# Output matmuls in two PSUM banks by column halves, with a second weight chunk kept on chip and 32-wide transposes

## The chip, the cores and the metric

The kernel runs on one core of a Trainium2 chip. The metric is the device time of one execution in microseconds (us); less is better. The engines of the core are TensorE (PE; its weight loads are listed apart as PEld), VectorE (DVE), ScalarE (ACT), GpSimd (POOL) and SyncE (SP). They run side by side and wait for each other on semaphores. SP and POOL issue the DMA transfers of this kernel's main loop.

## The reference

Two independent parts, whose outputs stand side by side. Part A is a long convolution through Fourier transforms; the change does not touch it. Part B is attention with a recurrent memory over 64 segments of 32 rows:

```
mem = mem0                                   # 8 rows of 1024
for s in range(64):
    h = concat(mem, x[32*s : 32*s+32])       # 40 rows
    q, k, v = h @ Wq, h @ Wk, h @ Wv         # 32 heads of 128
    p = softmax(mask(q @ k.T * scale))       # per head
    o = (p @ v) @ Wo                         # 40 rows of 1024
    mem, out[s] = o[:8], o[8:]
```

All four weights are 1024 x 4096 or 4096 x 1024 in bf16, 8 MB each, and each segment needs the memory rows that the segment before has produced. So every segment passes over all of the weights, and segments can't overlap.

## The kernel before

Part A and the work of part B that does not depend on the memory come first: keys, queries and values of the last 8 of each segment's 32 rows are prepared for all segments and left in DRAM (`REC`, `VBD`); the loop multiplies 32 rows by the K, Q and V weights, 8 of the memory and the segment's first 24. Then the loop over the 64 segments runs in an order written out by hand (`tc.manual_schedule()`), so each engine executes its instructions as the program lists them.

In a segment, the weights come as 64 chunks of 128 x 2048 (`order`): 8 each for K, Q, K, Q of the two groups of heads (`g`), 16 for V, and 16 for the output (`Wo`, one for each two heads). 47 of the chunks stay in SBUF; the other 17 (`STREAM`, places in `order`) are read from a DRAM copy `WS` through a ring of 6 buffers (`wring`). `done(ch)` frees a buffer after its last matmul and `fetch()` issues the next load on SP's queue. Two of the 17 are helped by unused columns of PSUM (`KEPT`): "A", an output chunk, lies there whole from the first segment on and is copied back quarter by quarter by VectorE (`quarter`, L817); "B", a key chunk, lies there to five eighths, is copied into its ring buffer by `move` (L800), and has its other three eighths loaded (L721).

The steps of one segment, in TensorE's order:

- `fill_mem` transposes the first half of the old output `Y` (L862) and VectorE copies its 8 memory rows into `hT` (in the tile `rec`, L863). Four key chunks follow, then the second half of `fill_mem`, then the other four.
- `Proj.run` (L918) multiplies a chunk: four matmuls of 512 columns, each with a 32-column stationary operand, side by side in four column tiles of the array. `evac` (L927, ScalarE) copies the result to SBUF as `qkv_sb` in a single buffer "rot".
- `transposes` (L933) turns a 128 x 512 result with four 128 x 128 transposes, and VectorE or ScalarE copies the result into `KT` or `QT`. `scores`, `softmax_a`, `softmax_b` and `attend` follow.
- `out_proj` and `project` (L1002) multiply with Wo: a chunk is four matmuls of 512 columns with a 64-column stationary operand, two side by side, all into one PSUM bank `yacc`, which takes its turn with the accumulators of the projections in a pool of two.
- ScalarE copies `yacc` to `Y` in two halves (L1078), and POOL writes the output rows to DRAM with two transfers (L1080).

The pool `one` has a single buffer for each tag. The tag "PT" is held in turn by `PT` (the transposed probabilities, read by `attend`) and by `Y`. The tag "QT" is held by `QT`, by the attention output `OT` of the first group and by every second quarter of A.

POOL also issues the load of the next segment's `rec` (L856, after the last projection) and of `VBs` (L889), and copies small operands for the scores (L893, L900).

Of the kernel before, what the change touches and what calls it, by code (L numbers as in the profile page):

```python
# [20 lines left out]

STREAM = (0, 5, 10, 15, 21, 26, 31, 36, 41, 46, 49, 52, 54, 57, 60, 61, 63)
KEPT = {14: "A", 4: "B"}
K0_ORDER = (0, 1, 4, 5, 2, 3, 6, 7)
# [3 lines left out]
X_LOAD = 1  # L28
RING = 6
LATE_SLOT = 4  # L30

# [385 lines left out]
def b_kernel(ctx: ExitStack, tc, x, mem0, Wq, Wk, Wv, Wo, outb, n_seg, run_a):  # L417
    nc = tc.nc
# [15 lines left out]
    for g in range(2):  # L434
        order += [(2, kc, g) for kc in range(8)]
    for hp in range(16):
        order.append((3, hp, 0))
# [257 lines left out]
    def more(i):  # L695
# [9 lines left out]
    loads = [(s, ch) for s in range(n_seg) for ch in order_s  # L705
             if s == 0 and ch not in v_temp[2:] or s > 0 and kept.get(ch) != "A"]
    live = {}
# [8 lines left out]
    def fetch():  # L716
        if loads:
            s, ch = loads.pop(0)
            live[s, ch] = k, t = slot()
            if s > 0 and ch in kept:  # L720
                nc.sync.dma_start(t[:, 0:768], stream_src(ch)[:, 0:768])  # L721
                move(kept[ch], t, True)
            else:
                nc.sync.dma_start(t[:], stream_src(ch))

# [13 lines left out]
    with c0p:  # L739
# [16 lines left out]
        for g in range(2):  # L756
# [14 lines left out]
            if g == 0:  # L771
                with tc.issue_after(got[-1].ins):
                    place_late(4, stage_home)
                    for i in [*range(len(v_temp) - 2, n_more), *range(len(v_temp) - 2)]:
                        place_late(1, lambda: more(i))
                    place_late(1, lambda: pw(2))
                    place_late(4, stage_home)
        assert len(late) == len(at_hand)

# [11 lines left out]
    OTi, tpi = OTp[:].bitcast(I32), tps[:].bitcast(I32)  # L791
    homes = {"B": [(OTi[:, :, 416:512], slice(384, 768)), (tpi[:, 1, :], slice(768, 1024))]}

    def move(name, t, back):
        for p, cols in homes[name]:
            w = t[:].bitcast(I32)[:, cols]
            if len(p.shape) == 3:
                w = w.rearrange("p (b x) -> p b x", b=4)
            src, dst = (p, w) if back else (w, p)
            nc.vector.tensor_scalar(out=dst, in0=src, scalar1=0, scalar2=None, op0=ALU.bitwise_or)  # L800

# [3 lines left out]
    def keep(ch):  # L805
        t = live[0, ch][1]
        if kept[ch] == "A":
            w = t[:].bitcast(I32).rearrange("p (hh dh f x) -> p hh f dh x", hh=2, dh=2, f=2)
            for q in range(4):
                nc.vector.tensor_scalar(out=OTi[:, q, 160:416].rearrange("p (dh x) -> p dh x", dh=2),  # L810
                                        in0=w[:, q // 2, q % 2], scalar1=0, scalar2=None, op0=ALU.bitwise_or)
        else:
            move(kept[ch], t, False)

    def quarter(q):
        t = one.tile([128, 512], BF, tag=("rot", "QT")[q % 2], name="quarter")
        nc.vector.tensor_scalar(out=t[:].bitcast(I32), in0=OTi[:, q, 160:416], scalar1=0, scalar2=None,  # L817
                                op0=ALU.bitwise_or)
        return [(o, o + 256, t[:, 256 * dh:256 * dh + 256]) for dh, o in enumerate(quarter_cols(q))]
# [14 lines left out]
    def done(ch):  # L834
        if now[0] == 0 and ch in at_hand:
            place_late(1, at_hand[ch][1])
        elif ch in streamed and (now[0] == 0 or kept.get(ch) != "A"):
            if now[0] == 0 and ch in kept:
                keep(ch)
            free.append(live.pop((now[0], ch))[0])  # L840
            i = order_s.index(ch)
            if now[0] == 0 and i == LATE_SLOT:
                free.append(2)
                fetch()
            fetch()
# [8 lines left out]
    def load_x(s):  # L854
        rec = one.tile([128, 768], BF, tag="rec", name="rec")
        nc.gpsimd.dma_start(rec[:], REC[:, s, :])  # L856
        pend[s] = (rec[:, 0:256].rearrange("p (k t) -> p k t", k=8), rec[:, 256:512], rec[:, 512:768])

    def fill_mem(hT, Y, half):
        tp = tps[:, 0, :]  # L860
        for j in (2 * half, 2 * half + 1):
            nc.tensor.transpose(tp[:, j * 128:(j + 1) * 128], Y[:, j * 128:(j + 1) * 128], ident[:])  # L862
        nc.vector.tensor_copy(  # L863
            hT.rearrange("p (dh j) t -> p dh j t", dh=2)[:, :, 2 * half:2 * half + 2, 0:NM],
            tp.rearrange("p (j dh r) -> p dh j r", j=4, dh=2)[:, :, 2 * half:2 * half + 2, 0:NM])

    with tc.manual_schedule():
        for _ in range(RING - 3):
            fetch()
# [14 lines left out]
        for s in range(n_seg):  # L884
# [19 lines left out]
            class Proj:  # L904


                def __init__(self, m, g):
                    self.m, self.g, self.kc = m, g, 0
                    self.acc = ps_acc.tile([128, 512], F32, tag="acc", name="acc")

                def run(self, n=8):
                    for n_kc in range(self.kc, self.kc + n):
                        kc = K0_ORDER[n_kc] if (self.m, self.g) == (0, 0) else n_kc
                        ch = (self.m, kc, self.g)
                        w = pieces(ch)
                        for c in range(4):
                            for x, y, r in columns(w, 512 * c, 512 * c + 512):
                                nc.tensor.matmul(self.acc[32 * c:32 * c + 32, x - 512 * c:y - 512 * c],  # L918
                                                 lhsT=hT[:, kc, :], rhs=r, start=(n_kc == 0 and x == 512 * c),
                                                 stop=(n_kc == 7), tile_position=(0, 32 * c))  # L920
                        done(ch)
                    self.kc += n
# [7 lines left out]
            def transposes(sb):  # L930
                tp = tps[:, 0, :]
                for i in range(4):
                    nc.tensor.transpose(tp[:, i * 128:(i + 1) * 128], sb[:, i * 128:(i + 1) * 128], ident[:])  # L933
                return tp.rearrange("p (i c r) -> p i c r", i=4, c=4)
# [59 lines left out]

            def project(h, w, OT):
                k = 40 * (h % 16)
                m = min(64, 640 - k)
                lhsT = OT[:].rearrange("p c i q -> p (c i q)")[:, k:k + m]
                for dh in range(2):
                    o = (h % 2) * 1024 + dh * 512  # L1000
                    for x, y, r in columns(w, o, o + 512):
                        nc.tensor.matmul(yacc[64 * dh:64 * dh + m, x - o:y - o], lhsT=lhsT,  # L1002
                                         rhs=r, start=(h == 0 and x == o), stop=(h >= 30),
                                         tile_position=(0, 64 * dh), skip_group_check=(h == 31))

            def out_proj(hps, OT):
                for hp in hps:
                    ch = (3, hp, 0)
                    if s > 0 and kept.get(ch) == "A":
                        continue  # L1010
                    w = pieces(ch)
                    for hh in range(2):
                        project(2 * hp + hh, w, OT)
                    done(ch)

            def out_quarter(q, w):
                hp = [ch[1] for ch in kept if kept[ch] == "A"][0]
                project(2 * hp + q // 2, w, OT1)

            fill_mem(hT, Y, 0)  # L1020
            k0 = Proj(0, 0).run(4)
            fill_mem(hT, Y, 1)
            k0 = k0.run(4).evac()
            q0 = Proj(1, 0).run(4)
# [3 lines left out]
            q0 = q0.run(4).evac()  # L1028
            k1 = Proj(0, 1).run(4)
            QT0 = one.tile([128, 4, 4, 32], BF, tag="QT", name="QT")  # L1030
            nc.vector.tensor_copy(QT0[:], transposes(q0))
            k1 = k1.run(4).evac()
            scores(0, QT0, KT0)
# [20 lines left out]
            V1 = pv1.evac()  # L1054
            yacc = ps_acc.tile([128, 512], F32, tag="acc", name="yacc")
            out_proj(range(0, 5), OT0)
            attend(1, PT1, V1)
            OT1 = evac_o(1)
            if s == 0:
                out_proj(range(5, 8), OT0)  # L1060
                out_proj(range(8, 16), OT1)
            else:
                w0 = quarter(0)
                out_proj(range(5, 8), OT0)
                w1 = quarter(1)
                out_quarter(0, w0)
                out_proj(range(8, 10), OT1)
                w2 = quarter(2)
                out_quarter(1, w1)
                out_proj(range(10, 12), OT1)  # L1070
                w3 = quarter(3)
                out_quarter(2, w2)
                out_proj(range(12, 14), OT1)
                out_quarter(3, w3)
                out_proj(range(14, 16), OT1)
            Y = one.tile([128, 512], BF, tag="PT", name="Y")
            for half in range(2):
                nc.scalar.copy(Y[:, 256 * half:256 * half + 256], yacc[:, 256 * half:256 * half + 256])  # L1078
            for dh in range(2):
# [73 lines left out]
```

## Time and profile before

| | |
|---|---|
| median of 3 runs | 1904.04 us (1904.03 to 1904.1) |
| the profiled execution | 1907.36 us, with a span of 1905.6 us from first to last instruction |
| granted TensorE clock over the span | 0.982 |
| TensorE busy | 1749.0 us, 92% of the span |
| VectorE, ScalarE, GpSimd busy | 853.8, 674.8 and 342.8 us |
| DMA | 678.00 MB, mean 356 GB/s; 373 GB/s from 600 us on |

The loop over the segments takes the span from about 450 us to the end. A profile row names the line, the engine, the operation, the tiles (out<-in), the count and times. In the chain of work that ended last, each row gives a start, a duration and what ran, and "issue" is time in which the engine waited for nothing that the profile shows. In the timeline, a row's second number is the time from the start of its first instruction to the end of its last; ends of matmuls are modelled and overlap the next one, so distances are read from start to start. In brackets stands the engine's idle time ahead of it and what ended that. In the rows of DMA issues, the last number is the median time from issue to landing.

### The profile page before, as it was taken

To read this page: it belongs to the slowest core of one execution; us is meant where nothing else is said; L and a number is where in the kernel's file an instruction comes from. 1 tells how busy PE (TensorE), PEld (TensorE's weight loads), DVE (VectorE), ACT (ScalarE), POOL (GpSimd) and SP (SyncE) were. 2 spreads that over 40 slices of the span, in tenths; PEclk is the share of its full clock that TensorE was granted. 3 is DMA by queue.
4 is the path that set the end of the run, shared out by engine and by line. 5 is a ranking of instruction groups with operands and counts; after the bars stand their busy time and mean duration, and the time that the engine had idled before them with its cause. 6 is when DMAs were issued, how large, how long until landed. Compare 5 with 4: busy or idle time off the path is not lost.

```text
span 1905.6 us, 62245 instructions
## 1 busy us (share of the span) xinstructions
PE 1749.0 (92%) x26353; PEld 831.1 (44%) x26353; DVE 853.8 (45%) x2812; ACT 674.8 (35%) x1195; POOL 342.8 (18%) x1014
## 2 busy tenths in 40 slices
PE   6989986778999999999999999999999999999998
PEld 3433322333444444444444444444444444444444
DVE  9927863202344444444444444444443444444443
ACT  6945640112333333333333333333333333333333
POOL 4003341000121111111121111111111111111111
PEclk9999998989999999999999999999999999999999
DMA  9989889998999999999999999999999999999998
GB/s 338 351 302 329 291 271 333 327 284 277 349 373 374 373 378 373 377 372 373 373 373 378 373 376 372 370 372 372 379 374 369 371 378 374 375 373 371 372 379 311
DMA packets 251211, 678.00 MB, mean 356 GB/s; under 512 B 74850, under 2 KB 82930, under 8 KB 250932
## 3 DMA queue, kind: packets, MB, share of 16 engines
q1 hardware_dynamic: 178692, 604.26, 85.0%
q0 software_dynamic: 17488, 46.70, 7.0%
q10 hardware_dynamic: 54752, 23.07, 4.5%
q8 instruction: 206, 3.38, 0.7%
q14 instruction: 73, 0.60, 0.1%
HBM read 618.35 MB, written 59.24 MB: 356 GB/s over the span
## 4 chain that ended last, share of the span: by engine, by line
PE 80%; DMA 7%; DVE 5%; issue 4%; ACT 2%; POOL 0%; ACTq 0%; SPq 0%; DVEq 0%; POOLq 0%
PE acc L918 38%; PE yacc L1002 22%; PE kb_ps L625 5%; PE tps L933 4%; DMA wring<-WS 3%; PE vb_ps L765 3%; DMA REC<-stage 2%; PE OTp L980 1%; ACT s_sb L243 1%; DVE rec L863 1%; PE SB L942 1%; PE tps L862 1%; PE s_ps L241 1%; DMA REC<-xt 1%; PE SB L939 1%
## 5 line engine op out<-in xcount | busy, mean ns | idle before, releaser
L918 PEld LDWEIGHTS <-rec 128*32 128x32 bf16 x12288 | 283.6, 96 | 300.2 <-DVE rec L863 60.7
L927 ACT CAST qkv_sb<-acc 128x512 bf16<-128x512 f32 x384 | 224.7, 585 | 480.0 <-PE acc L918 287.9
L1002 PEld LDWEIGHTS <-OT 128*64 128x64 bf16 x4348 | 255.1, 109 | 195.3 <-ACT OT L992 27.6
L918 PE MATMUL acc<-wring,rec 128*32 128x512 bf16 x2556 | 252.7, 382 | 22.8 <-DVE rec L863 19.1
L918 PE MATMUL acc<-Wres,rec 128*32 128x512 bf16 x3328 | 249.4, 380 | 0.6 <-issue 0.6
L1002 PE MATMUL yacc<-wring,OT 128*64 128x512 bf16 (+1 forms) x1540 | 235.9, 380 | 5.0 <-DMA wring<-WS 4.9
L918 PE MATMUL acc<-Wmid,rec 128*32 128x512 bf16 x3072 | 234.4, 382 | 0.0
L1002 PE MATMUL yacc<-Wmore,OT 128*64 128x512 bf16 (+1 forms) x1280 | 185.4, 381 | 0.0
L817 DVE TENSOR_SCALAR quarter<-OTp 128x256 int32<-128x256 int32 x252 | 101.1, 422 | 187.6 <-ACT OT L992 149.3
L1080 POOL DMA_DIRECT2D out_dram<-Y x128 | 63.7, 502 | 484.5 <-ACT Y L1078 484.2
L918 PE MATMUL acc<-pw,rec 128*32 128x512 bf16 x1796 | 144.8, 382 | 0.1
L1078 ACT CAST Y<-yacc 128x256 bf16<-128x256 f32 x128 | 41.4, 375 | 274.5 <-PE yacc L1002 274.5
L992 ACT CAST OT<-OTp 128x640 bf16<-128x640 f32 x128 | 88.6, 692 | 129.7 <-PE OTp L984 129.0
L918 PE MATMUL acc<-Wlate,rec 128*32 128x512 bf16 x1280 | 104.0, 384 | 17.1 <-DVE rec L863 17.1
L948 DVE TENSOR_REDUCE mx<-SB 128x5 f32<-128x200 f32 x128 | 47.1, 368 | 153.4 <-PE SB L942 153.3
L856 POOL DMA_DIRECT2D rec<-REC x64 | 36.2, 566 | 405.0 <-PE acc L918 372.1
L1002 PE MATMUL yacc<-Wlate,OT 128*64 128x512 bf16 x768 | 105.7, 383 | 0.2 <-ACT OT L992 0.2
L933 PEld LDWEIGHTS <-qkv_sb 128*128 128x128 bf16 x1024 | 57.8, 97 | 109.5 <-ACT qkv_sb L927 108.0
L933 PE MATMUL tps<-ident,qkv_sb 128*128 128x128 bf16 x1024 | 101.6, 222 | 0.4 <-ACT qkv_sb L927 0.3
L893 POOL COPY KT<-rec 128x128 bf16<-128x128 bf16 x128 | 38.2, 298 | 329.4 <-PE SB L942 324.2
L863 DVE COPY rec<-tps 128x32 bf16<-128x32 bf16 x128 | 22.3, 175 | 165.1 <-PE tps L862 115.8
L1027 DVE COPY KT<-tps 128x512 bf16<-128x512 bf16 x64 | 27.1, 424 | 152.2 <-PE tps L933 152.2
(215 smaller groups left out, 2392.9 us busy)
## 6 DMA issues: line engine op xcount, KB each, us to landing
wring<-WS SPq DMA_DIRECT2D x961, 512.0 KB, 6.0
rec<-REC POOLq DMA_DIRECT2D x64, 192.0 KB, 5.8
wring<-WS SPq DMA_DIRECT2D x63, 192.0 KB
SK<-s_sb SPq DMA_DIRECT2D x16, 512.0 KB, 4.8
SU<-s_sb SPq DMA_DIRECT2D x16, 512.0 KB, 4.9
Kg<-SK SPq DMA_DIRECT2D x32, 256.0 KB, 4.2
Ug<-SU SPq DMA_DIRECT2D x32, 256.0 KB, 5.7
REC<-stage ACTq DMA_DIRECT2D x16, 512.0 KB, 10.9
```

Of the source, the lines that this page charges most:

```text
L625: nc.tensor.matmul(ps[:], lhsT=ws[kc][:, hl * 128:(hl + 1) * 128], rhs=xbt(kc).rearrange("p s t -> p (s t)"), start=(kc == 0), stop=(kc == 7))
L765: nc.tensor.matmul(ps[:], lhsT=xbt(kc)[:, 16 * tb:16 * tb + 16, :].rearrange("p s t -> p (s t)"), rhs=ws[kc][:, c * 512:(c + 1) * 512], st ...
L817: nc.vector.tensor_scalar(out=t[:].bitcast(I32), in0=OTi[:, q, 160:416], scalar1=0, scalar2=None, op0=ALU.bitwise_or)
L863: nc.vector.tensor_copy(hT.rearrange("p (dh j) t -> p dh j t", dh=2)[:, :, 2 * half:2 * half + 2, 0:NM], tp.rearrange("p (j dh r) -> p dh ...
L918: nc.tensor.matmul(self.acc[32 * c:32 * c + 32, x - 512 * c:y - 512 * c], lhsT=hT[:, kc, :], rhs=r, start=(n_kc == 0 and x == 512 * c), st ...
L927: nc.scalar.copy(sb[:], self.acc[:])
L933: nc.tensor.transpose(tp[:, i * 128:(i + 1) * 128], sb[:, i * 128:(i + 1) * 128], ident[:])
L948: nc.vector.tensor_reduce(out=mx[:], in_=S, op=ALU.max, axis=AX.X)
L992: nc.scalar.copy(OT[:], o_view)
L1002: nc.tensor.matmul(yacc[64 * dh:64 * dh + m, x - o:y - o], lhsT=lhsT, rhs=r, start=(h == 0 and x == o), stop=(h >= 30), tile_position=(0, ...
L1078: nc.scalar.copy(Y[:, 256 * half:256 * half + 256], yacc[:, 256 * half:256 * half + 256])
L1080: nc.gpsimd.dma_start(bass.AP(outb.tensor, outb.offset + SEG * s * 2048 + 512 * dh, [[2048, 32], [1, 512]]), Y[64 * dh + NM:64 * dh + 40, :])
```

## The change

- *Output in two banks.* `yacc` becomes two tiles of the same pool of two, one for each half of the 512 columns. Each output matmul has 256 columns. The first four chunks and the last four run half by half: all four with the first half (f = 0), then all four with the second. `Y`'s first half is copied after the last four chunks' f = 0.
- *Handover.* The next segment's `fill_mem` half 0 is issued before the last chunk's f = 1. Half 1 comes after three key chunks instead of four.
- *32-wide transposes.* `turn_tile` does a 128 x 128 transpose as four, each in one of the four column tiles. `fill_mem` and `transposes` use it.
- *Chunks.* 48 chunks are resident instead of 47; the new one takes a buffer of the ring, which now has 5. 16 are streamed in the first segment; after that both kept chunks lie in PSUM (B with a quarter of a quarter in an SBUF tile `B_rest`), so that 14 are loaded per segment. B is no longer copied into a ring buffer: VectorE copies four parts of it (`quarter_b`) into the tags "PT", "QT", "PT" and "rot", and they are multiplied as four pieces between the other chunks of the second key projection.
- Between two quarters of A stands one output chunk instead of two. The places in `STREAM` and the order of the output chunks (`O_ORDER`) differ, and the copy of `QT0` moves from VectorE to ScalarE.

```diff
-STREAM = (0, 5, 10, 15, 21, 26, 31, 36, 41, 46, 49, 52, 54, 57, 60, 61, 63)
-KEPT = {14: "A", 4: "B"}
+STREAM = (1, 7, 13, 18, 20, 24, 30, 35, 41, 46, 49, 53, 56, 59, 60, 62)
+KEPT = {13: "A", 4: "B"}
+FIRST, LAST = (0, 1, 2, 3), (15, 11, 12, 14)
+O_ORDER = (*FIRST, 4, 5, 6, 7, 8, 9, 10, 13, *LAST)
-RING = 6
+RING = 5
...
+        place_late(1, lambda: base.tile([128, 2048], BF, tag="wring2", name="Wring"))
...
+    B_rest = one.tile([128, 4, 32], I32, name="B_rest")
+    B_homes = [tpi[:, 1, :].rearrange("p (c x) -> p c x", c=4),
+               SB[:].bitcast(I32)[:, 200:456].rearrange("p (c x) -> p c x", c=4),
+               OTi[:, :, 416:480], OTi[:, :, 480:512]]
+    def bits(dst, src):
+        nc.vector.tensor_scalar(out=dst, in0=src, scalar1=0, scalar2=None, op0=ALU.bitwise_or)
+    def quarter_b(q, tag):
+        n = 64 if q < 3 else 32
+        t = one.tile([128, 4, 2 * n], BF, tag=tag, name="quarter_b")
+        bits(t[:].bitcast(I32), B_homes[q])
+        w = [(512 * c + 128 * q, 512 * c + 128 * q + 2 * n, t[:, c, :]) for c in range(4)]
+        if q == 3:
+            w += [(512 * c + 448, 512 * c + 512, B_rest[:].bitcast(BF)[:, c, :]) for c in range(4)]
+        return w
...
+    def turn_tile(dst, src):
+        for e in range(0, 128, 32):
+            nc.tensor.matmul(dst[e:e + 32, :], lhsT=src[:, e:e + 32], rhs=ident[:], start=True, stop=True,
+                             is_transpose=True, tile_position=(0, e))
...
-            def project(h, w, OT):
+            def project(h, f, w, OT, stop=False):
...
-                    o = (h % 2) * 1024 + dh * 512
-                    for x, y, r in columns(w, o, o + 512):
-                        nc.tensor.matmul(yacc[64 * dh:64 * dh + m, x - o:y - o], lhsT=lhsT,
+                    o = (h % 2) * 1024 + dh * 512 + f * 256
+                    for x, y, r in columns(w, o, o + 256):
+                        nc.tensor.matmul(yacc[f][64 * dh:64 * dh + m, x - o:y - o], lhsT=lhsT,
...
-            fill_mem(hT, Y, 0)
-            k0 = Proj(0, 0).run(4)
+            if s == 0:
+                fill_mem(hT, Y, 0)
+            k0 = Proj(0, 0).run(3)
             fill_mem(hT, Y, 1)
-            k0 = k0.run(4).evac()
+            k0 = k0.run(5).evac()
...
-            k1 = Proj(0, 1).run(4)
+            k1 = Proj(0, 1)
+            if s > 0:
+                kb = [ch[1] for ch in kept if kept[ch] == "B"][0]
+                b0, b1 = quarter_b(0, "PT"), quarter_b(1, "QT")
+                k1.run(1)
+                k1.add(kb, b0)
+                b2 = quarter_b(2, "PT")
+                k1.run(2)
+                k1.add(kb, b1)
+            else:
+                k1.run(4)
             QT0 = one.tile([128, 4, 4, 32], BF, tag="QT", name="QT")
-            nc.vector.tensor_copy(QT0[:], transposes(q0))
-            k1 = k1.run(4).evac()
+            nc.scalar.copy(QT0[:], transposes(q0))
+            if s > 0:
+                b3 = quarter_b(3, "rot")
+                k1.run(3)
+                k1.add(kb, b2)
+                k1.add(kb, b3)
+            k1 = k1.run(8 - k1.kc).evac()
...
-            yacc = ps_acc.tile([128, 512], F32, tag="acc", name="yacc")
-            out_proj(range(0, 5), OT0)
+            yacc = [ps_acc.tile([128, 512], F32, tag="acc", name="yacc") for f in range(2)]
+            for f in range(2):
+                for hp in FIRST:
+                    out_half(hp, f, OT0)
+            out_proj((4,), OT0)
...
             Y = one.tile([128, 512], BF, tag="PT", name="Y")
-            for half in range(2):
-                nc.scalar.copy(Y[:, 256 * half:256 * half + 256], yacc[:, 256 * half:256 * half + 256])
+            for f in range(2):
+                for hp in LAST:
+                    if f == 1 and hp == LAST[-1] and not last:
+                        fill_mem(pend[s + 1][0], Y, 0)
+                    out_half(hp, f, OT1, hp == LAST[-1])
+                nc.scalar.copy(Y[:, 256 * f:256 * f + 256], yacc[f][:, 0:256])
```

## The prediction

> **What bounds the kernel now.** I read the granted clock first (0.982 over the span, 1.00 in the segment loop), then the chain of work that ended last, cut to one segment (22.5 us; 64 of them take three quarters of the span).
>
> ```profile
> 1041.91 0.39 PE yacc L1002 x3
> 1042.30 0.89 issue
> 1043.19 0.19 DVE rec L863
> ...
> 1043.42 1.05 PE acc L918 x16
> 1044.46 0.23 PE tps L862 x2
> ...
> 1044.72 0.18 DVE rec L863
> ...
> 1044.95 1.91 PE acc L918 x32
> 1046.86 0.33 PE tps L933 x4
> ```
>
> Nearly everything in it is TensorE (PE). It stands still only where a segment hands over to the next: output out of PSUM, transpose, copy into the stationary operand (`rec`), twice. The timeline gives issue times:
>
> ```profile
> 1041.72 0.62 PE L1002 MATMUL yacc<-wring,OT 128*64 128x512 bf16 x4
> 1042.38 0.65 ACT L1078 CAST Y<-yacc 128x256 bf16<-128x256 f32 x2 [4.20 <-PE yacc L1002]
> 1043.32 1.00 POOL L1080 DMA_DIRECT2D out_dram<-Y  x2 [7.33 <-ACT Y L1078]
> 1046.47 0.39 PE L918 MATMUL acc<-Wmid,rec 128*32 128x512 bf16 x4
> 1046.79 0.40 PE L933 MATMUL tps<-ident,qkv_sb 128*128 128x128 bf16 x4
> 1047.12 0.61 PE L918 MATMUL acc<-Wmid,rec 128*32 128x512 bf16 x8
> 1061.22 0.30 PE L1002 MATMUL yacc<-quarter,OT 128*64 128x256 bf16 x2
> 1061.33 0.62 PE L1002 MATMUL yacc<-Wmore,OT 128*64 128x512 bf16 x4
> 1061.76 0.62 PE L1002 MATMUL yacc<-wring,OT 128*64 128x512 bf16 x4
> ```
>
> Pairs of 512 columns are 0.215 us apart (x4 in 0.43), four 32-wide ones 0.217. A chunk issued at 1046.47 should be followed at 1046.69; the transposes come at 1046.79: 0.10 us lost where the array's tiling changes. Then the DMA answers: the loop from 600 us on, and the last microseconds, where nothing else is moved.
>
> ```profile
> wring<-WS SPq DMA_DIRECT2D x860, 512.0 KB, 6.0
> out_dram<-Y POOLq DMA_DIRECT2D x114, 32.0 KB, 4.8
> out_dram<-Y POOLq DMA_DIRECT2D x2, 32.0 KB, 1.7
> ```
>
> SP's queue takes 94.7% of the engines there, yet TensorE waits for a load 2.6 us in all from 500 to 1900: TensorE bounds, the DMA is close behind. An output write lands 4.8 us after its issue in this traffic (5.4 at most from 1000 to 1500), 1.7 alone.
>
> **Part by part, per segment.** *Handover.* The last pair is issued at 1041.94 (second of the x4), so the next chunk was due at 1042.16 and comes at 1043.42: 1.26 us. The second transposes delay it again: due at 1043.42 + 4 x 0.217 = 1044.29, issued at 1044.95: 0.66. Together 1.92. In the changed order the first half of `Y` is copied while the second half's matmuls run. Left are: `fill_mem` half 0 among the last matmuls (two groups of four transposes, 0.06 each, and two changes of tiling, 0.10 each: 0.31); the change to the keys, 0.10; half 1, 0.11, and the wait for its copy: the old one resumed 0.55 after its transposes began, the new one needs some 0.45 and has 0.11 + one chunk (0.22) to do: 0.12. Sum 0.64. The second copy of `Y` (0.375) and its hand-over lie under the three chunks of `run(3)`, 0.65; gone, they would cost up to 0.6. Gain 1.28.
>
> *32-wide transposes.* The four of L933 hold TensorE from 1046.69 to 1047.12, 0.43. As 16 in four column tiles, the tiling of the matmuls around, they are four groups of 0.057 ((0.33 - 0.10)/4): 0.23. Gain 0.20 x 4 = 0.80. That the transpose flag alone costs no such change no row shows; bounds 0 and 0.80, and I take 0.80, because entering the attention and output tilings (no flag) costs the same 0.10.
>
> *Column halves.* 64 pairs of 256 columns for 32 of 512. The row is the quarter: 1061.22 to 1061.33, 0.11 against 0.1075 for half a pair; at most 0.15 in sum, and I take 0.05. The second bank is the one of `V1`: its first matmul comes 8 x 0.108 = 0.87 after the first half's, the copy of `V1` (1057.45 to 1058.03, with the first output matmul at 1057.28) and its hand-over end 0.81 after: covered by 0.06. [...]
>
> *Chunk B from PSUM.* 20 small matmuls for 4: +0.02. Four DVE copies of about 0.42 replace two (0.56, 0.41); behind the first, the second is done 0.42 later and needed two chunks (0.43) later, and the fourth, which waits for the transposes to free its buffer, comes some 0.05 late. The quarters of A lie closer: between two stand a chunk and a pair, 0.54, where a copy (0.42) with its drain and hand-overs takes about 0.6: +0.05. Moving the `QT0` copy to ScalarE lies under the rest of `k1`. Together, with what the halves cost, some 0.2. TensorE's gain is 1.28 + 0.80 - 0.20 = 1.88, and 0.07 more: the mean segment is 22.59 (first to last output write), the common one 22.52, and the waits between them belong to the tight loads.
>
> *A new wait.* `quarter_b(0)` writes the buffer of `Y` (tag PT), and so waits on VectorE until both output writes have landed. Before, PT's next writer came 5 us later (softmax). Queued behind it on VectorE are the other quarters and softmax; TensorE waits for it in `k1`, and the `k1` copy on ScalarE waits for TensorE. Call E the issue of the segment's first key matmul. TensorE needs the quarter after 17 chunks (3.69), transposes (0.23) and half 1 (0.23): E + 4.15. The last pair is issued at E - 0.21; the copy of `Y` starts 0.33 after (1041.94 to 1042.38, less the shorter stream) and takes 0.375: E + 0.50. POOL issues 0.29 later (1043.03 to 1043.32), its second write 0.5 after that: E + 1.29. With a landing time W, the quarter's 0.41 and two hand-overs of 0.06, it is ready at E + 1.82 + W. TensorE waits W - 2.33.
>
> So a segment changes by W - 2.33 - 1.95 = W - 4.28 us. W is what decides. Bounds: 1.7 (alone) and 5.4 (longest). Loads in flight now: 6.0 landing over 22.5/15.4 = 1.46 per load, 4.1. In the changed order the ring has five slots and 14 loads per segment, and around E three are in flight (slots of order places 60 and 62 and of the second key chunk, freed at about E - 1.0, E - 0.6, E + 0.4; the one before, at E - 3.3, has landed). In proportion W = 1.7 + 3.1 x 3/4.1 = 4.0, which I take. With 1.5 loads ahead it is 2.8, with as many as now 4.8 to 5.0. [...] The row of 4.8 shows two loads' worth of delay, so the sum keeps the rows' proportion.
>
> *Loads.* 14 x 0.524 + 0.33 MB = 7.67 MB per segment at the 373 GB/s of the page: 20.6 us, the same as TensorE without the wait (22.59 - 1.95 = 20.6). The loads bind only if the wait vanishes. The 48th resident chunk costs one more load in the first segment, and saves a staging copy: zero, give or take 3 us in all.
>
> **Sum.** 63 x (4.0 - 4.28) = -18 us. The profiled execution took 1907.4 (span 1905.6 and 1.8 around), 3.3 above the median. 1907.4 - 18 - 3.3 = **1886**.
>
> **Rivals.** *The output write decides* (slower): W stays as now, 4.95 for the second write; 63 x 0.67 = +42, 1946. For it: the writes still fall into a burst of loads. Against: fewer in flight. It decides from W = 4.34. *No wait*: W at or below 2.3; then 20.6 per segment, -123, 1781. For it: 1.7 alone; against: the burst at E. *The flag keeps the tiling change*: three of the four blocks lie behind the wait, 3 x 0.20 x 63 = +38 on the forecast, 1924.
>
> **Chances.** Forecast 0.58 (W from 2.8 to 4.3: of it 0.06 within 0.2%), first rival 0.22 (0.01 within), second 0.10, third 0.10 (0.01 within). Faster 0.62, same 0.08, slower 0.30; 0.2%, 3.8 us, is about what a measurement of this kernel can tell from no change. The forecast's own range is W 2.8 to 4.3: 1811 to 1905. The range to 8 in 10 leaves out the second rival and W above 5: 1815 to 1946.
>
> **What would show it.** Right: a group of VectorE `quarter_b` copies whose idle time ends with the landing of out_dram, some 1.7 us a time, TensorE waiting for `quarter_b` as much; transposes of 0.23 with no 0.10 ahead; no pause at the handover above 0.2; pairs of 256 columns 0.108 apart. Wrong: no idle time ahead of `quarter_b` (then 1781), or more than 2.1 (then slower); 0.10 around the new transposes; halves at 0.13 or more (64 x 0.02 x 63 = +80).

## The result and the profile after

| | before | changed kernel |
|---|---|---|
| median | 1904.07 us | 2167.44 us (2158.81 to 2180.83, 4 runs) |
| ratio to before | | 1.138 (1.132 to 1.144) |
| profiled execution, its span | 1907.36, 1905.6 us | 2180.83, 2179.1 us |
| granted clock, span | 0.982 | 0.911 |
| mean segment in the profiled run | 22.59 us | 26.85 us |

The prediction said 1886 us, 1815 to 1946. The kernel became slower, by more than the range allowed. In the profiled run 4.26 us were lost in each of 63 segments, 268 us in all; the two medians differ by 263 us.

The chain of work that ended last, cut to one segment (start, duration, what ran), shows where:

```profile
1017.23 0.23 PE tps L864 x8
1017.46 0.36 PE yacc L1013 x4
1017.84 0.38 ACT Y L1113
1018.22 0.28 issue
1018.51 0.45 POOL out_dram L1115
1019.01 6.11 DMA out_dram<-Y
...
1025.24 0.44 DVE quarter_b L796
1025.72 1.26 PE acc L922 x16
```

Before, this chain was nearly all TensorE. Now it leaves TensorE at the copy of `Y`, goes through the output write, and comes back only when VectorE has copied the first part of chunk B. The waits (engine, line, what it waited for: us in total, times, longest) and the DMA issues give the sizes:

```profile
DVE quarter_b L796 <- DMA out_dram<-Y: 239.7, 62, 5.6
PE acc L922 <- DVE quarter_b L796: 231.4, 62, 5.4
```

```profile
wring<-WS SPq DMA_DIRECT2D x818, 512.0 KB, 5.5
...
out_dram<-Y POOLq DMA_DIRECT2D x116, 32.0 KB, 6.3
```

This is the wait that the prediction named, at the place it named, 3.7 us a time in place of 1.7. The write lands 6.3 us after its issue; it was 4.8 before, and the sum had taken 4.0. In the timeline:

```profile
1017.79 0.40 PE L922 MATMUL acc<-Wlate,rec 128*32 128x512 bf16 x4
...
1018.51 1.02 POOL L1115 DMA_DIRECT2D out_dram<-Y  x2 [7.56 <-ACT Y L1113]
...
1021.90 0.39 PE L922 MATMUL acc<-Wmid,rec 128*32 128x512 bf16 x4
...
1025.24 0.42 DVE L796 TENSOR_SCALAR quarter_b<-tps 128x256 int32<-128x256 int32 x1 [3.56 <-DMA out_dram<-Y]
...
1025.72 0.30 PE L922 MATMUL acc<-quarter_b,rec 128*32 128x128 bf16 x4 [3.43 <-DVE quarter_b L796]
...
1025.78 0.67 PE L922 MATMUL acc<-Wmid,rec 128*32 128x512 bf16 x4
...
1026.20 0.67 PE L922 MATMUL acc<-wring,rec 128*32 128x512 bf16 x4
```

E is 1017.79; TensorE reaches the part of B at about E + 4.3, as forecast (4.15), and gets it at E + 7.93. The last two rows show a second cost: the chunk after the pause is followed 0.42 us later, where 0.217 was usual before. The windows (TensorE's busy time and count, then the other engines', then the granted clock, DMA share and GB/s) say why:

```profile
1019.00:1022.00 3.00, 2.98 (x68) 1.62 (x69) 0.42 (x1) 0.59 (x1) 1.94 (x8) 1.00 0.96 284
1022.00:1025.70 3.70, 0.29 (x8) 0.00 (x0) 0.46 (x2) 0.59 (x1) 0.00 (x0) 0.87 0.97 372
1025.70:1029.00 3.30, 3.28 (x60) 1.91 (x63) 1.01 (x3) 0.59 (x1) 0.00 (x0) 0.50 0.61 227
1029.00:1032.00 3.00, 3.00 (x80) 1.71 (x76) 2.17 (x9) 1.14 (x3) 0.90 (x5) 0.57 0.47 156
1032.00:1035.00 3.00, 3.00 (x100) 1.59 (x96) 0.82 (x6) 1.88 (x4) 0.00 (x0) 1.00 0.72 261
```

In this segment the granted clock is still 1.00 from 1022.30 to 1024.73, 2.4 us into the pause, and 0.50 from there to 1031.55, so 5.8 us of work after the pause run at half. Over 59 segments of the loop the stretches at half last 3.41 us (21 of them) or 6.83 us (33), 5.0 us a segment in the mean; a few pauses bring none. The longer of the two is twice the shorter. What sets these lengths, and why the clock fell 2.4 us into this pause, no run here shows.

### The profile page after: what moved, and what is told of

Same layout as the page of the kernel before. It is cut to its first block, busy times and chain, and to the rows that moved or that the text cites. A ratio compares the mean times of both kernels' runs of the same rounds, so it can differ in the third digit from the quotient of the medians.

```text
span 2179.1 us, 79472 instructions
## 1 busy us (share of the span) xinstructions
PE 1834.5 (84%) x35013; PEld 1083.3 (50%) x35045; DVE 864.7 (40%) x2877; ACT 718.4 (33%) x1259; POOL 344.9 (16%) x1013
## 4 chain that ended last, share of the span: by engine, by line
PE 64%; DMA 24%; DVE 4%; ACT 3%; issue 2%; POOL 2%; ACTq 1%; DVEq 0%; another core or an unknown queue 0%; POOLq 0%; SPq 0%
PE acc L922 26%; PE yacc L1013 22%; DMA out_dram<-Y 19%; PE kb_ps L626 4%; PE tps L864 3%; DMA REC<-stage 2%; PE vb_ps L762 2%; POOL out_dram L1115 1%; DVE quarter_b L796 1%; PE OTp L991 1%; ACT s_sb L244 1%; ACT Y L1113 1%; DMA VBD<-pair 1%; PE SB L953 1%; PE s_ps L242 1%
## 5 line engine op out<-in xcount | busy, mean ns | idle before, releaser
L922 PEld LDWEIGHTS <-rec 128*32 128x32 bf16 x13296 | 341.1, 105 | 539.1 <-issue 328.5
L1013 PEld LDWEIGHTS <-OT 128*64 128x64 bf16 (+1 forms) x8192 | 433.2, 109 | 53.2 <-ACT OT L1003 27.4
L922 PE MATMUL acc<-Wmid,rec 128*32 128x512 bf16 x3072 | 305.3, 461 | 0.0
L922 PE MATMUL acc<-quarter_b,rec 128*32 128x128 bf16 x1008 | 63.2, 274 | 232.9 <-DVE quarter_b L796 232.9
L1013 PE MATMUL yacc<-wring,OT 128*64 128x256 bf16 (+1 forms) x2568 | 236.5, 274 | 2.9 <-DMA wring<-WS 2.4
L1013 PE MATMUL yacc<-Wmore,OT 128*64 128x256 bf16 (+1 forms) x3072 | 233.2, 273 | 0.0
L1055 ACT COPY QT<-tps 128x512 bf16<-128x512 bf16 x64 | 37.5, 587 | 297.3 <-PE tps L864 297.3
L864 PEld LDWEIGHTS <-qkv_sb 128*32 128x32 bf16 x4096 | 85.1, 110 | 83.2 <-ACT qkv_sb L938 47.1
L796 DVE TENSOR_SCALAR quarter_b<-tps 128x256 int32<-128x256 int32 x63 | 26.8, 425 | 241.3 <-DMA out_dram<-Y 241.3
L864 PE MATMUL tps<-ident,qkv_sb 128*32 128x128 bf16 x4096 | 119.7, 243 | 0.2 <-ACT qkv_sb L938 0.2
```

Of the source, the lines that this page charges most:

```text
L864: nc.tensor.matmul(dst[e:e + 32, :], lhsT=src[:, e:e + 32], rhs=ident[:], start=True, stop=True, is_transpose=True, tile_position=(0, e))
L1013: nc.tensor.matmul(yacc[f][64 * dh:64 * dh + m, x - o:y - o], lhsT=lhsT, rhs=r, start=(h == 0 and x == o), stop=stop, tile_position=(0, 64 ...
```

## Experiments

The letters name questions, not the order in which the kernels ran. "Stops" in what follows are counted in the trace's loop (59 segments): a TensorE matmul that starts over 0.4 us after the one before it, with no releaser in the profile ("issue"), in excess of the usual 0.216. Segments are means unless the text says median.

**A. What sets the landing time?** `half_loads`: from the third segment on every streamed load brings half of its columns, and the matmuls use that half twice.

```diff
-            nc.sync.dma_start(t[:], stream_src(ch))
+            if s > 1:
+                nc.sync.dma_start(t[:, 0:1024], stream_src(ch)[:, 0:1024])
+            else:
+                nc.sync.dma_start(t[:], stream_src(ch))
...
+        if now[0] > 1:
+            return [(0, 1024, t[:, 0:1024]), (1024, 2048, t[:, 0:1024])]
```

> The changed kernel, but from the third segment on each load of a weight chunk brings half of its columns, and the matmuls of the other half read the first one: half of the streamed weights are left out. If the output write lands late because five loads are queued ahead of it, its landing falls from 6.4 to 3 or 3.5 us, TensorE's wait to under 1 us, and the kernel takes 1800 to 1860. If the lateness belongs to the write's own path (POOL's queue, the write receipt), the landing stays above 5.5 and the kernel above 2080.

Measured: 1895.46 us (one run), above the 1800 to 1860 that I gave. The writes land 3.2 and 3.6 us after issue (medians) in place of 6.3 and 6.4, the pause at `quarter_b` is 54 us in 59 segments in place of 220, and the loop's clock is 0.99. With half the bytes queued beside it, the write's landing time fell to about half.

`writes_first`: the same loads, three of them issued behind the writes.

```diff
+            if behind:
+                nc.gpsimd.memset(t[:, 0:2], 0.0)
             nc.sync.dma_start(t[:], stream_src(ch))
...
+            while held:
+                held.pop()
+                fetch(True)
```

> The changed kernel with its wait for the output writes as it is, but the three loads whose buffers come free around the handover (order places 60, 62 and the next segment's place 1) are issued behind the two output writes: GpSimd writes two columns of each buffer after it has issued the writes, and the load waits for that. Theory (the landing time W of the writes is set by the loads queued ahead of them, five where the prediction counted three): with two ahead, W falls from 6.4 to 3.0 to 3.8, VectorE's wait ahead of quarter_b from 3.7 to 0.4 to 1.1 us, the granted clock in the loop returns from 0.91 to 0.98 or more; the late loads cost 0.2 to 1.0 of waits for wring and instruction blocks 0.5 to 1.5 of stops: segment 22.4 to 24, kernel 1900 to 2000. Rival (W is long for another reason, such as the queue that GpSimd uses): W stays at 5.5 or more and the kernel at 2100 or more.

```profile
wring<-WS SPq DMA_DIRECT2D x802, 512.0 KB, 5.9
...
out_dram<-Y POOLq DMA_DIRECT2D x116, 32.0 KB, 2.0
```

Measured: 2025.11 us, ratio 1.064 (1.060 to 1.067), segment 24.44, clock in the loop 1.00; the kernel and the segment are both above what I gave. The writes land after 2.0 us, less than expected, though the loads still take 5.9. So here the loads issued just ahead of the writes set W (2.0 with three of them moved behind, 6.3 with them ahead), and without them VectorE's wait ahead of `quarter_b` is gone as a cost (0.2 us a segment). What came instead is 1.1 us a segment of waits for the delayed loads, a little more than expected, and 1.48 us of stops, at the upper end.

`out_on_act`: the writes issued by ScalarE.

```diff
-                nc.gpsimd.dma_start(bass.AP(outb.tensor, ...
+                nc.scalar.dma_start(bass.AP(outb.tensor, ...
```

> The changed kernel with one edit: the two output writes are issued by ScalarE instead of GpSimd. Theory (loads ahead set W, whoever issues): the writes are issued a little earlier, 0.3 to 0.5 us, but land as late after it, W 5.5 to 6.5, kernel 2110 to 2180. Rival (GpSimd's queue makes the writes late): W 2 to 4, the wait ahead of quarter_b under 1.5, kernel 1900 to 2020.

Measured: 2090.8 us (2089.58 to 2092.02), ratio 1.098, a little below the range that I gave. TensorE's wait for `quarter_b` falls from 231 to 185 us (62 times each), 0.74 a segment, of which the earlier issue (0.4 and 0.76 us after the copy of `Y` starts, for 0.67 and 1.16) explains 0.3 to 0.4. The queue is at most a small part of W; the trace gives no landing time for these writes, so this is read from the wait alone.

**B. What is left if the wait goes?** `other_buffer`: the first and third part of B lie in the buffer of `E`, made large enough.

```diff
-                b0, b1 = quarter_b(0, "PT"), quarter_b(1, "QT")
+                b0, b1 = quarter_b(0, "E"), quarter_b(1, "QT")
...
-                b2 = quarter_b(2, "PT")
+                b2 = quarter_b(2, "E")
```

> The changed kernel, with the two parts of chunk B that went into the buffer of Y (tag PT) put into the buffer of the softmax tile E (made 1024 bytes per partition wide). Theory 1, the wait: the loss is TensorE waiting for the landing of the output writes (3.7 us a segment) and the slower clock after that pause; without the shared buffer both vanish, the segment takes 20.6 to 20.9 us, the kernel 1780 to 1800, the granted clock in the loop is 1.0. Theory 2, the forms: 256-column halves and 32-wide transposes with their many more weight loads run slower and pull the clock down by themselves; then the kernel stays above 2050 us and the clock near 0.9. Theory 3, the loads: with the wait gone the 14 loads per segment bind; 20.6 us at the 373 GB/s of before and waits on wring, 1800 to 1840.

Measured: 2000.91 us, ratio 1.050 (1.046 to 1.053), segment 23.99, clock in the loop 0.99. The wait for the output write is gone, and it was worth 167 us. But the kernel is still slower than before, and none of the three theories gave this time. The waits of TensorE now have at their head rows with no releaser:

```profile
PE acc L922 <- issue: 52.9, 39, 3.0
PE tps L864 <- issue: 18.1, 13, 2.2
PE acc L922 <- DMA wring<-WS: 14.2, 28, 1.6
PE SB L953 <- issue: 14.1, 12, 1.9
```

and in the timeline such a stop stands in the middle of a group of matmuls whose operands are all there:

```profile
1020.04 0.22 PE L950 MATMUL SB<-KT,QT 128*32 128x40 bf16 x4
1021.30 0.20 PE L953 MATMUL SB<-KT,QBm 128*32 128x40 bf16 x4 [1.04 <-issue]
1021.34 0.19 PE L950 MATMUL SB<-KT,QT 128*32 128x40 bf16 x4
```

Three things in the trace say that TensorE waits for its own instructions. The "instruction" queue (q8) carries packets of 16 KB; a DMA row of 600 to 1800 us gives their number, the megabytes and the share of the engines, first for the kernel before and then for `other_buffer`:

```profile
q8 instruction: 161, 2.64, 0.9%
```

```profile
q8 instruction: 204, 3.34, 1.1%
```

A segment of `other_buffer` has 520 matmuls, 520 weight loads and 2 semaphore instructions on TensorE, and 59 segments bring 240 packets: 256 instructions each. A packet ran from 1018.80 to 1019.73, and TensorE went on at 1021.30; all 95 stops of this run's loop end so, 1.43 us (1.29 to 1.57 for nine in ten) after the end of a packet. And where a segment follows a segment, the stop moves 9 matmuls towards the segment's start (195th, 186th, 177th, 168th, 159th, 150th in six segments running): 1042 instructions are four packets and 18 instructions more, nine matmuls with their loads. (The counts below leave the 2 out: 1040.) How many such packets TensorE holds at a time, no run here shows.

`warm`: the pause filled with 132 small matmuls whose results aren't used.

```diff
                 k1.run(1)
+                for n in range(33):
+                    for c in range(4):
+                        nc.tensor.matmul(OTp[32 * c:32 * c + 32, c, 0:160], lhsT=hT[:, 0, :], ...
                 k1.add(kb, b0)
```

> The changed kernel, with 132 extra matmuls of 160 columns (33 groups of four, some 2.2 us) ahead of the first part of chunk B, where TensorE otherwise pauses; their results go to a place that attend overwrites. Theory 1 (the wait, and a slower clock because of the pause): the wait ends when it did, the pause is cut from 3.7 to about 1.5 us, the clock in the loop goes from 0.91 to 0.99 or 1.0, a segment takes 24.5 instead of 26.8, the kernel about 2020. Theory 2 (the forms pull the clock down): 2.2 us more work per segment at the same clock, 2167 or more, up to 2300.

Measured: 2238.27 us, ratio 1.176 (1.173 to 1.178). The loop's clock rises from 0.906 to 0.956, but the 264 extra instructions bring 2.54 us of stops a segment, most of them within the added matmuls. The pause shrinks as meant (TensorE waits for `quarter_b` 28 us in 59 segments), and the time lies in the range of theory 2; but the stops, which neither theory has, make it so, and the run does not decide between the two. `other_buffer` does: the same forms without the pause, at a clock of 0.99.

`other_buffer_wide`: `other_buffer` with 128-wide transposes.

```diff
-        for e in range(0, 128, 32):
-            nc.tensor.matmul(dst[e:e + 32, :], lhsT=src[:, e:e + 32], rhs=ident[:], ...
+        nc.tensor.transpose(dst, src, ident[:])
```

> As other_buffer, with the 128-wide transposes of before instead of the 32-wide ones. If the 32-wide ones save the change of tiling (0.20 us for each of four blocks, and about 0.1 at the handover), this is 0.8 to 1.0 us a segment slower than other_buffer, 50 to 60 us in all. If the transpose flag costs the change of tiling anyway, or the loads bind, the two are within 15 us.

Measured: 1929.28 us, ratio 1.013 (1.011 to 1.015). The transposes cost more time on TensorE, and the kernel is 72 us faster than `other_buffer`: the opposite of what I expected. It has 920 instructions a segment for 1040, and its stops are 0.52 us a segment for 1.99. Many instructions and many stops went together, and that made the instruction fetch the theory to test.

**C. Why do the instructions come late?** `other_buffer_half` has all instructions of `other_buffer` and half of the loaded bytes (the edit of `half_loads`).

> Built on other_buffer (the parts of chunk B in the buffer of E, so nothing waits for the output writes). From the third segment on each load brings only the first half of a chunk's columns, and the matmuls use that half twice: the second half of the streamed weights is left out. The instruction streams of all engines are those of other_buffer, 1040 TensorE instructions per segment. Theory (a 16 KB block of instructions is fetched late because it queues behind the weight loads): the stops without a releaser, 2.1 us a segment in other_buffer, shrink to the 0.2 that half_loads shows, the segment falls from 23.9 to 20.6 to 21.0, the kernel to 1780 to 1815 us. Rival (so many short instructions cannot be supplied or issued faster, whatever the DMA does): the stops stay at 2 us a segment, only the 0.3 of waits for loads goes, segment 23.6, kernel about 1980.

The windows of the two, `other_buffer` first:

```profile
1000.00:1500.00 500.00, 455.42 (x10895) 294.67 (x10888) 200.00 (x774) 169.12 (x314) 80.80 (x290) 0.99 0.91 323
```

```profile
1000.00:1500.00 500.00, 498.07 (x12261) 324.96 (x12250) 226.74 (x880) 192.00 (x356) 90.97 (x328) 1.00 0.59 191
```

Measured: 1830.94 us (one run), segment 21.27 (median 21.20). TensorE goes from 455 to 498 of 500 us busy with the same instruction stream, and one stop is left in 59 segments. So 1040 instructions a segment can be supplied and issued; it is the loads beside them (323 GB/s, landing after 5.9 us) that make their blocks late. The segment is longer than the 20.6 to 21.0 I gave; more of that below.

`before_narrow`: the kernel before with 32-wide transposes alone; `before_narrow_half`: the same with half loads.

```diff
-                    nc.tensor.transpose(tp[:, i * 128:(i + 1) * 128], sb[:, i * 128:(i + 1) * 128], ident[:])
+                    turn_tile(tp[:, i * 128:(i + 1) * 128], sb[:, i * 128:(i + 1) * 128])
```

> The kernel before with one part of the change alone: the 20 transposes of a segment as 80 of 32 rows, 888 TensorE instructions per segment for 768. Prediction's step: 4 tiling changes of 0.20 go, 63 x 0.80 = 50 us, 1854. Instruction-fetch theory: the gain of 0.80 stays in the rows, but 888 instructions lie between before (768, 0.13 us of stops a segment) and other_buffer_wide (920, 0.59), at about 0.45, so 0.8 - 0.3 = 0.5 remains, 1870 to 1885. Rival (32-wide transposes are themselves slower in this traffic, as other_buffer_wide being 72 us faster than other_buffer could be read): slower than before, 1920 or more.

> before_narrow (the kernel before with 32-wide transposes alone, 1958 us) with the loads cut: from the third segment on each streamed chunk brings only half of its columns, used twice, so half of the streamed weights is left out (chunk B is moved and loaded as before). TensorE's instructions are those of before_narrow. Theory (the 32-wide transposes do save TensorE time, and instruction blocks that come late behind the loads take more than that back): the stops of 1.5 us a segment fall to 0.2 or less, and the segment is shorter than the 22.5 of the kernel before by 0.5 to 0.8: 21.7 to 22.1, the kernel 1845 to 1880. Rival (the many small transposes are slow by themselves): segment 22.6 or more, the kernel 1910 or more.

Measured: 1958.45 us, ratio 1.029 (1.027 to 1.032), with 1.31 us of stops a segment; and 1857.88 us (one run), median segment 21.74, with three stops in all. I had expected `before_narrow` to gain, and it lost 54 us. For the stops I had put 0.45. With half loads the common segment falls from 22.52 to 21.74, by 0.78: all 20 transposes together, where the prediction's 0.80 was for the 16 of the four groups alone. (The kernel before was not run with half loads; its waits for loads are 0.05 us a segment.) Under full loads the change costs more than it saves: 888 instructions beside 15.4 loads a segment stop TensorE 74 times in 59 segments, and 768 (the kernel before) once.

`other_buffer_ring4` and `wide_ring4`: one ring buffer left unused.

```diff
-    free = [4, 5, 0, 1, 3]
+    free = [4, 5, 0, 1]
...
-        for _ in range(RING - 2):
+        for _ in range(RING - 3):
```

> other_buffer (32-wide transposes) with one ring buffer left unused. Fetch theory: the stops of 2.1 us a segment shrink by a fifth to a half, to 1.1 to 1.7, while waits for loads grow from 0.28 to 0.3 to 0.8: segment 23.2 to 23.9, kernel 1955 to 2000. Rival (the queue has no part in it): stops stay at 2.1, and the kernel is at 2000 to 2030.

> other_buffer_wide with one ring buffer left unused, so four loads are queued at most instead of five; nothing else differs. Fetch theory: fewer loads ahead of each instruction block, the stops of 0.59 us a segment shrink to 0.3 or less; the loads themselves have one buffer less of lead, so the waits for loads (0.29 a segment) may double. Net from -0.3 to +0.3 a segment, 1910 to 1950, and the two parts are to be read apart in the trace. Rival (stops do not depend on the queue): they stay at 0.59 and the waits grow, 1940 or more.

Measured: 2016.96 us, ratio 1.060 (1.057 to 1.062), and 1989.91 us, ratio 1.044 (1.042 to 1.047). The stops fell from 1.99 to 1.05 and from 0.52 to 0.08 us a segment, as the theory has it: a shorter queue of loads, earlier instructions. The waits for loads rose from 0.3 to 1.5 a segment in both, where I had allowed 0.8 at most, and took more than the gain: both kernels are slower than I gave.

**D. Is there a version faster than both?** `last_halves`: only the last four output chunks half by half, f = 1 of them in the second bank and added by VectorE; 128-wide transposes; parts of B as in `other_buffer`; 832 instructions. `last_halves_mem`: 32-wide transposes for the memory rows alone; 856.

```diff
+                    new = f == 1 and h // 2 in LAST
...
+                    Yh = one.tile([128, 256], F32, tag="E", name="Yh")
+                    nc.scalar.copy(Yh[:], yacc[0][:, 256:512])
+                else:
+                    nc.vector.tensor_tensor(out=Y[:, 256:512], in0=yacc[1][:, 0:256], in1=Yh[:], op=ALU.add)
```

> A version meant to beat both: the changed kernel's handover and both chunks in PSUM with the parts of B in the buffer of E, but 128-wide transposes, and only the last four output chunks half by half. The other chunks go with 512 columns into one bank; the last four add f = 0 to its first half and put f = 1 into the second bank, and VectorE adds that to the second half, which ScalarE has copied to E's buffer. About 830 TensorE instructions per segment, for 920 in other_buffer_wide. Theory: TensorE alone needs what it needs in other_buffer_wide (22.0 without its stops), the stops fall from 0.59 to some 0.3, the waits for loads stay at 0.3: segment 22.4 to 22.6, 1890 to 1910. Rival (the number of instructions isn't what makes the stops): 0.6 stays, 22.9, 1929.

> last_halves with 32-wide transposes for the four memory tiles only (24 instructions more per segment, about 855). They save tiling changes at the handover, some 0.2 to 0.4 us a segment by the rows of other_buffer_half, where all 20 tiles save 0.7 to 0.9; the stops may grow by 0.1 to 0.3 as their instructions lie close together. Segment 22.2 to 22.6, kernel 1875 to 1910. If the stops come from the narrow transposes above all, it is slower than last_halves.

Measured: 1920.93 us, ratio 1.009 (1.007 to 1.011), and 1915.37 us, ratio 1.007 (1.005 to 1.009). Both beat the changed kernel by about 250 us, and neither beats the kernel before. Both are above the range that I gave for them. The stops stayed at 0.53 and 0.48 us a segment, though there are 88 and 64 instructions less than in `other_buffer_wide`. So the rival I gave for this run held: over this range the number of instructions alone doesn't set the stops.

| kernel | TensorE instructions per segment | loads | stops, us per segment | mean segment |
|---|---|---|---|---|
| before | 768 | full | 0.01 | 22.59 |
| `last_halves` | 832 | full | 0.53 | 22.72 |
| `before_narrow` | 888 | full | 1.31 | 23.47 |
| `before_narrow_half` | 888 | half | 0.01 | 21.81 |
| `other_buffer_wide` | 920 | full | 0.52 | 22.88 |
| `other_buffer` | 1040 | full | 1.99 | 23.99 |
| `other_buffer_half` | 1040 | half | 0.01 | 21.27 |
| changed kernel | 1040 | full | 0.05 | 26.85 |

The last row is worth a second look: the changed kernel has the same 1040 instructions, and next to no stops. Taking the pause away brought them out (`other_buffer`, 1.99 us), and so did filling it (`warm`, 2.54); here one wait hid another. That the pause gives the fetch time to come up is the reading; fewer bytes are moved beside it too (285 GB/s for 323).

The first row may owe something to place. The kernel before runs 770 instructions a segment with the 2 for semaphores, three packets and 2 instructions more (177 packets in 59 segments), so the boundaries between its blocks of 256 move by one matmul a segment; in `other_buffer` they move by nine, and in `last_halves`, `before_narrow` and `other_buffer_wide` by more. No run parts this from the number of instructions.

## Why the prediction was wrong

Per segment, the forecast was W - 4.28 = -0.28 us, and +4.26 came. The difference of 4.5 has three parts; the first is the step that failed, and the largest. The mechanism, a wait of VectorE for the output write, was the one named.

**The landing time W (the step that failed).** The prediction took W = 4.0, from "three are in flight" and in proportion to the 4.8 of the kernel before. It was 6.3 for the first and 6.4 for the second write (medians), above both ends that it had kept (1.7 and 5.4). The count was low: in the changed kernel's trace the ring's five loads are issued 4.9, 3.4, 1.0 and 0.6 us ahead of `Y`'s second copy and 0.6 after it. The first of them has just landed when the first write is issued, 0.7 us after that copy starts; the other four are in flight, among them the one that was said to have landed. And the proportion failed with the count: four loads give 4.7 by it and five 5.5, and the kernel before has five in flight at its first write (issued 5.5, 4.2, 2.8, 1.2 and 0.3 ahead of the copy, the fourth of 192 KB) and lands it after 4.7. What differs is the burst: three of the changed kernel's loads are issued within 1.6 us just ahead of the write. `writes_first` moves these three behind the writes and has 2.0; `half_loads` halves the loads and has 3.2 and 3.6. So the loads just ahead set W; that they count for more because most of their bytes are still to come is a reading. By the prediction's own formula W = 6.4 gives a wait of 4.1 for 1.7; measured were 3.9 from start to start. So the formula held, and its input did not: +2.2 us.

**The clock after the pause (a term that was missing).** The mean segment is 26.85; without pause and stops it is 21.27 (`other_buffer_half`), and the pause is 3.9: 1.7 us are left. The trace has room for them: outside the pauses the clock is at 0.50 for 4.2 us a segment, worth 2.1 at most. It stays a remainder, since `warm`, which was to part pause and clock, brought stops of its own. In the segment shown above it was more, 27.63 from copy to copy less 21.2 and the pause's 3.6: 2.8. The prediction costed a wait at its length. With the pauses of `half_loads` (1.0 us each) the loop's clock is 0.99, with the 3.0 of `out_on_act` 0.95, with the changed kernel's 3.7 it is 0.91.

**TensorE's gain was over-stated.** Forecast was 1.88, of the common 22.52; `other_buffer_half` has 21.20, a gain of 1.32. The distances from start to start (medians over 55 segments) divide it:

| | before | `other_buffer_half` | gain | forecast |
|---|---|---|---|---|
| handover | 1.92 | 0.88 | 1.04 | 1.28 |
| transposes, four groups | 1.71 | 1.02 | 0.69 | 0.80 |
| the rest | 18.89 | 19.30 | -0.41 | -0.20 |

Of the handover's 0.88, half 0 among the last matmuls is 0.35 (0.31 forecast), the step to the keys 0.19 (0.10), the transposes of half 1 are 0.11 as forecast, and the wait for its copy is 0.24 (0.12). In the rest lie two waits around chunk B: 0.16 behind its second part, where the transposes wait for ScalarE's copy of the first query projection, and some 0.15 ahead of its fourth, whose copy comes late behind the transposes (0.05 forecast); and the waits for the quarters of A (0.05 and 0.10). The halves were right: 0.109 us a pair, two weight loads in it, as the quarter's row of 0.11 had it.

**What was not in the sum at all** is the instruction fetch. It costs the changed kernel little, and it would have made the second rival ("no wait, 1781") wrong too: with the wait gone the kernel takes 2000.91. The prediction counted what each added instruction takes on TensorE. It did not count that 272 more of them per segment (1040 for 768) are to be fetched by the DMA engines that it had called "close behind"; the q8 row (0.9% of the engines) was in the profile before.

**Rivals.** The first, the output write decides, named the mechanism and the sign; its 1946 rested on W as before. The third, that the transpose flag keeps the tiling change, is out: in `before_narrow_half` a group of 16 holds TensorE for 0.23 us, as forecast, and no 0.10 stands ahead of it.

What stays open: why `last_halves` stops as often as `other_buffer_wide` with fewer instructions, which places in the stream can wait for a block without cost, and how much of the quiet of the kernel before is due to such places. That the stops come at the ends of packets and vanish with half the loads is shown; that the packets queue behind loads on the same engines is the reading that fits both, and was not seen packet by packet.

## What to carry to other kernels

Here a buffer shared with the source of a DMA tied the next writer to that DMA's landing (VectorE waited 239.7 us for it, 62 times), and the landing moved with the loads issued just ahead of it (6.3 us, and 2.0 with three of them behind the writes). So list the loads in flight at that moment from the trace, with those issued just ahead of it, and take the queue's full depth where you can't. Where TensorE waits as long as here (3.7 us in the mean), cost the half clock after it too (5.0 us a segment at 0.50). And where the DMA engines are as busy as here (a share of 0.91 in `other_buffer`), count the instructions: splitting matmuls into smaller ones cost next to nothing on TensorE's own rows (0.109 us a pair of halves for 0.1075), and yet the 1040 instructions of a segment came with 1.99 us of stops, for 0.01 with half the loads. So try the kernel with half the loads to see what the order of work is worth by itself.

## What the hardware showed that I had not expected

- Pauses of TensorE of 3.7 us (mean) bring stretches of 3.41 or 6.83 us at a granted clock of 0.50, 5.0 us in the mean segment, and the one in the segment shown begins 2.4 us into the pause; the pauses of up to 0.9 us at the handover before left the clock at 1.00.
- TensorE stands still with no releaser in the profile, and its next matmul starts 1.4 us after the end of a 16 KB packet of instructions: 95 times in 59 segments at 1040 instructions and 323 GB/s (`other_buffer`); at 191 GB/s (`other_buffer_half`) one stop is left.
- An output write of 32 KB takes 2.0 us with three loads moved behind it and 6.3 with them ahead, while the loads' own landing time (5.9 and 5.5) hardly differs.
